# Sketched attention into a SiLU layer on one core: V loads on two queues, a new instruction order, and last chunks that come out token-major

## The chip, the core and the metric

The kernel runs on one core of a Trainium2 chip. The metric is device time in microseconds of one execution. Before the change it is 100.06 us, the median of four runs (98.99, 99.80, 100.32, 102.11). The profile shown is of the execution that took 98.99 us. Engines are called PE (TensorE matmul), PEld (its weight loads), DVE (VectorE), ACT (ScalarE), POOL (GpSimd) and SP (SyncE, which here only issues DMAs); ACT issues DMAs too, on a queue of its own.

## The reference

Four batches, four heads, 1088 tokens, head size 32. Attention without softmax: queries and keys are each projected by two 8 x 32 sketches, and the outer product of the two 8-vectors is a 64-vector of features. The result, as 4352 tokens of 128 values, goes through a layer of 2048 units with SiLU.

```python
def phi(x):
    a = np.einsum('rd,bhsd->bhsr', S1, x)
    b = np.einsum('rd,bhsd->bhsr', S2, x)
    return np.einsum('bhsi,bhsj->bhsij', a, b).reshape(*x.shape[:-1], r * r)
q_p, k_p = phi(q), phi(k)
kv = np.einsum('bhsf,bhsd->bhfd', k_p, v)
z = np.sum(k_p, axis=2)
num = np.einsum('bhsf,bhfd->bhsd', q_p, kv)
den = np.einsum('bhsf,bhf->bhs', q_p, z)[..., None] + 1e-06
x = (num / den).transpose(0, 2, 1, 3).reshape(4352, 128)
h = x @ w_in
out = (h / (1 + np.exp(-h))) @ w_out
```

## The kernel before

**Attention, per batch.** Of a batch's 1088 tokens, 1024 are eight blocks of 128 and 64 are a rest. K, Q and V are loaded by token groups (`load_x`, `load_k`, `load_v`, L174 to L192); four DMAs bring the V of one batch, one for each 32-partition group (c = 0 to 3). DVE transposes K and Q in 32 x 32 blocks (`KT`, L299; `QT`, L524, L527 and L594), PE projects them with masked sketch weights (L268), DVE transposes the projections back (`kab`, L316; `qabm`, L546, L618), and DVE or POOL forms the outer products (`kp`, L322; `qp`, L462, L638). V is cast to bf16 (`vcast`, which ends in `copy`, L161 on ACT and L163 on other engines). PE sums key features times V over the tokens (`kv0`, L350, for batch 0; `kv`, L372, for the others), and a masked copy of the sum is the key-value matrix `KV` (`kvm0`, L361 on ACT; `kvm`, `kvt`, `kvc` for the others). The denominator is folded into the queries: `z` (L328), `zt`, `l2` (L336) and `wm` (L340) make a matrix `WM`, `projm` (L539, L606) applies it, and the scale group (L454 to L457, or L630 to L633) multiplies, sums, inverts and scales. The query features are transposed, in batch 0 by PE (`pet`, L483, four 128 x 128 blocks with a copy `qt` after them), in the others by DMA (`dmat`, L644). The numerator matmul (L496, L650, L658) gives the attention result with its 128 values on the partitions, copied to `xT` (eight blocks) or `xR` (the rest of all batches).

**The layer.** `moe_tasks` (L708) takes a chunk of 512 or 256 tokens. For each piece of units, `h` (L718) fills a PSUM tile `H` of 128 x 1024, `silu` (L722, ACT) makes a bf16 tile `G` of it, and `o` (L729) adds `w_out` times `G` into one bank, with the 128 output values on the partitions. There are 68 such pieces. At a chunk's end `tro` (L734, DVE) transposes the bank in 32 x 32 blocks and the store writes it in four DMAs of 32 values (128 bytes) per row (`store_main`, L690); the rest of all batches, 256 tokens, goes out in eight (`store_rest`, L700). Chunks are called m, batch, first block: m34 and m36 are the last two of batch 3, of 256 tokens each, and mR is the rest. There are two `H` tiles, four other PSUM banks (`B`) and eight `G` tiles.

**What sets the order.** Every piece of work is a task of the class `Plan` (L45), with an engine or a choice of engines, a planned cost, tasks it depends on, and PSUM or `G` buffers that it takes and gives back. The text `ORDER` lists all task numbers by hand, with a `.n` where an engine is chosen. `replay` goes through the list with the planned costs, only to decide which free buffer each task gets; `emit` writes the instructions in the list's order, and each engine runs its own in that order, without overtaking. Where a planned PE gap ahead of the first `h` is left, `fill` (L837) puts matmuls of zeros there. SP runs its DMA issues in order too; eight DMA semaphores are used in turn, so an issue waits until the transfer that had its semaphore before has landed.

**Loads at the start.** SP issues K in four parts, Q in two, the four V loads, the next batch's K, the two halves of w_in, the first quarter of w_out and the next Q; the other quarters of w_out follow with later loads. The weights come as fp32 and are cast to bf16 in quarters by POOL or ACT (`cast_w`). ACT issues the two sketch loads (L200) ahead of its table load and a small warm-up activation.

```python
vc = [pl.add(("ACT", "POOL"), (...), lambda e, lo=lo, hi=hi: vcast(e, lo, hi), lv, ...)
      for lo, hi in ((0, CUT), (CUT, NBX))]
```

Each of the two casts of batch 0's V depends on all four loads (`lv`).

Of the kernel before, what the change touches and what calls it, by code (L numbers as in the profile page):

```python
# [9 lines left out]
FP32 = mybir.dt.float32  # L10
BF16 = mybir.dt.bfloat16
ACT = mybir.ActivationFunctionType
# [3 lines left out]
ORDER = """  # L16
0 6 73 27 24 1 28 23 2.1 21 3.1 29 32 22 4 96 30 33 7 5 31 10 34 39.1 15 41.0 36 101 35 54 49 47.0
74 55 50 51 57 75 45.1 43.0 52 58 25.0 56 77 37.0 78 76 59 26.0 60 42 38 142 40 44 61.0 13 46 48
139 66 53.1 67 62 141 97 63.0 9.0 17 103 8.1 68.1 64 99 104 65.0 100 19 79 11.0 225 80 98 228 226
12.0 144 69 182 105 229 140 70.1 86.1 231 143 107 71 106 232 234 81.1 72.1 87 121 113 235 239 14.0  # L20
114 82 240 88.1 108.0 242 83.1 115 89 227 146 16.0 90.0 84 245 116 110.0 85.0 147 122 243 123 111.0
124 246 253 125 18.0 241 126 254 244 127 248 247 249 102.0 230 256 148 130.0 257 20.0 259 128.0 233
131 260 236 250 237 109.0 262 129 251 265 149 263 255 112.0 150 258 238 145.0 152.1 266 117 164 156
118.1 268 151.0 119 252 271 269 120.0 261 190 91.1 264 272 189 154.0 134 184 274 136.1 137.0 183
267 155.0 185 157 270 275 153.1 186 279 132.1 273 280 276 305 277 158 306 282 159 278 191 283 165
193 285 192 167 308 198.0 286 166 168 160 309 169 199 170 288 161.1 307 200 289 311 310 312 281
171.0 291 284 292 173.0 314 172 162 287 315 317 197.0 174 290 318 294 293 295 133 201 320 202 313
163.1 194.1 321 323 187 196.1 316 319 324 195.0 297 177 298 188.0 326 180.1 296 327 179.1 300 322
175.0 301 207 325 331 299 332 334 92 302 335 93.1 357 303 208 358 304 135 360 211 328 210 361 363
329 209 364 337 330 212 359 338 213 366 94 333 367 176 340 336 341 95.1 343 218.0 216.0 203 219 344  # L30
369 339 204.0 370 217 214.0 346 362 347 205 349 206.0 215 138.1 342 350 372 365 373 221 178 375
181.1 224.1 345 376 409 368 410 412 220 413 378 222.1 371 379 223.1 352 411 353 414 383 374 384 386
348 387 389 377 390 380 392 381 385 393 395 382 351 396 398 354 399 401 355 388 402 404 356 391 405
415 394 416 397 423 400 424 426 403 427 418 406 419 429 407 417 430 437 408 420 438 440 421 425 441
422 432 428 433 443 431 444 446 434 447 439 435 442 436 445 448 449 450
# [9 lines left out]
class Plan:  # L45
# [29 lines left out]
    def replay(self, seq):  # L75
        now, mode, queue, port = dict(self.now), None, 4.2, 0.0
# [42 lines left out]
def kernel(  # L119
# [11 lines left out]
    nc = tc.nc  # L131
# [129 lines left out]
    def dma(kb, fn, deps=(), issue=0.44, lag=1.6, due=None, ready=0.0, eng="SP", rate=330.0, name=""):  # L261
        return pl.add(eng, issue, fn, deps, lag=lag, due=due, ready=ready, dq=kb / rate, name=name)
# [9 lines left out]
    def load(b):  # L272
# [13 lines left out]
        ks[b]["lv"] = [dma(139, lambda c=c: load_v(nc.sync, b, c), dv, due=at + 0.5, rate=250.0, name=f"lv{b}{c}") for c in range(4)]  # L286
        qs[b]["lq"] = dma(557, lq, dq, due=at + 1.0, name=f"lq{b}")

    def key_tasks(b, cuts):
# [102 lines left out]
        if b == 0:  # L392
            lv = [dma(139, lambda c=c: load_v(nc.sync, 0, c), due=5.0 + 0.1 * c, rate=250.0, name=f"lv0{c}") for c in range(4)]
# [46 lines left out]
        else:  # L440
            k1 = pl.add("PE", 0.42, kv, ou + vc, take=("s",), mode="32", name=nm("kv"))
            t = pl.add(("DVE", "ACT"), (0.23, 0.32), kvm, [k1], name=nm("kvm"))
            t = pl.add("PE", 0.12, kvt, [t], name=nm("kvt"))
# [142 lines left out]
    def query_tasks_hm(b):  # L586
# [94 lines left out]
        n0 = pl.add("PE", 0.32, num, dm[0:2] + [kst["kvd"]], take=("s", "s"), mode="64", name=nm("num"))  # L681
        n1 = pl.add("PE", 0.09, numr, [dm[2], kst["kvd"]], take=("s",), mode="64", name=nm("numr"))
        st["nums"] = [n0, n1]
        st["xs"] = [pl.add(both, (0.6, 0.62), lambda e, g=g: xcopy(e, g), [n0], give=[(n0, g)], name=nm(f"x{g}")) for g in range(2)]
        st["x8"] = pl.add(both, (0.28, 0.22), xrest, [n1], give=[(n1, 0)], due=T0 + STEP * (16 * b + 12), name=nm("xr"))

    def store_main(b, a0, na, queues):
        def f(ot):
            for r in range(4):
                queues[r % len(queues)].dma_start(  # L690
                    AP(tensor=out.tensor, offset=out[b * S + a0, 32 * r].offset,
                       ap=[[SA * DM, 32], [DM, na], [1, 32]]),
                    ot[32 * r: 32 * (r + 1), 0: 32 * na].rearrange("p (a y) -> p a y", y=32))
        return f

    def store_rest(ot):
        o = ot[:, 0: B * XN].rearrange("p (b c y) -> p b c y", c=NX, y=32)
        for r in range(4):
            for c in range(NX):
                nc.sync.dma_start(  # L700
                    AP(tensor=out.tensor, offset=out[4 * NB + c, 32 * r].offset,
                       ap=[[SA * DM, 32], [S * DM, B], [1, 32]]),
                    o[32 * r: 32 * (r + 1), :, c, :])
# [4 lines left out]
    def moe_tasks(x, n, xdeps, store, nst=4, tag=""):  # L708
# [15 lines left out]
        def o(jp, sl=None):  # L724
            if jp == 0:
                cc["o"] = sl
            for i in range(J):
                j = J * jp + i
                nc.tensor.matmul(cc["o"][:, :n], w_out[:, j, :], view(cc["g", jp], i),  # L729
                                 start=(j == 0), stop=(j == NJ - 1))  # L730
# [139 lines left out]
```

## Time and profile before

| What | Value |
|---|---|
| median of four runs | 100.06 us |
| profiled execution: its time / its span | 98.99 / 96.9 us |
| granted PE clock, mean | 0.982 |
| ACT: 68 SiLU tiles (L722) | 65.0 us, 1032 ns each |
| PE: `h` (L718) x160 / `o` (L729) x176 | 37.8 / 37.6 us |
| DVE / POOL busy | 58.3 / 29.8 us |
| chain of waits: PE / DVE share | 72% / 8% |
| DMA queue of SP: packets, data | 30240, 12.72 MB |
| output stores: 24 of 64 KB, 16 of 32 KB, 8 of 16 KB | 2.0, 1.7 to 1.8, 1.6 us to landing |

The page has busy times by engine, the busy share in 40 slices (2.4 us each), and the chain of waits, which follows the work that ended last back to the start. The timeline gives for each row its start and duration in us from the span's start, the engine (a `q` behind it means that its sequencer issues a DMA), the line, and the operation with its tiles as out<-in; `x4` means four instructions run together, and the bracket shows how long the engine stood idle before, and what ended that. Matmuls overlap, so the time of a matmul group is best read from the chain, where each piece counts once.

### The profile page before, as it was taken

The page shows a single profiled execution, that of the slowest core. Times are in us where ns is not written, and L with a number is a line of the kernel's source. Part 1 is how long each engine was busy: PE and PEld are TensorE (multiplying, and loading weights), DVE is VectorE, ACT ScalarE, POOL GpSimd, SP SyncE. Part 2 cuts the span into 40 slices and gives each one's busy share as a digit, 9 for nine tenths or more (in the row PEclk, how much of TensorE's full clock was granted, in tenths as well). Part 3 has the DMA queues.
Part 4 walks back from the last instruction along what each step waited for, and adds up shares of the span by engine and source line. Part 5 has one row for each costly group of instructions (what it writes and reads, how often), then busy time and mean ns, then how long its engine had stood idle before and what let it go on. Part 6 is the DMA issues. An engine that isn't in the chain of part 4 may idle for free.

```text
span 96.9 us, 2290 instructions
## 1 busy us (share of the span) xinstructions
PE 87.4 (90%) x879; PEld 51.5 (53%) x879; DVE 58.3 (60%) x146; ACT 71.9 (74%) x88; POOL 29.8 (31%) x41
## 2 busy tenths in 40 slices
PE   5998779999998699999999999999999999999600
PEld 4565369693755344454454443454564447799400
DVE  4586999977999997489953678992040220210200
ACT  3310176998587579888999998999999999999200
POOL 5029319799299995069000000000000000000000
PEclk9999999999999999999999999999999999999975
DMA  1999999999982854941086506727300166053151
GB/s 37 247 264 234 309 404 336 296 231 250 277 265 74 153 93 70 227 69 31 0 167 120 194 0 108 112 54 151 72 0 0 20 99 98 0 82 59 28 82 27
DMA packets 30874, 12.93 MB, mean 133 GB/s; under 512 B 26256, under 2 KB 29072, under 8 KB 30864
## 3 DMA queue, kind: packets, MB, share of 16 engines
q1 hardware_dynamic: 30240, 12.72, 56.2%
q8 instruction: 7, 0.11, 0.5%
q10 hardware_dynamic: 624, 0.07, 0.5%
q14 instruction: 3, 0.02, 0.1%
HBM read 8.79 MB, written 2.23 MB: 114 GB/s over the span
## 4 chain that ended last, share of the span: by engine, by line
PE 72%; DVE 8%; issue 1%; DVEq 0%
PE H L718 30%; PE B L729 27%; PE B L268 4%; DVE qp L638 4%; PE B L837 2%; PE B L372 1%; DVE aqs L633 1%; PE B L328 1%; PE B L606 1%; PE B L650 1%; PE B L483 1%; PE B L496 1%; DVE ot L734 1%; DVE den L631 1%; PE H L350 1%
## 5 line engine op out<-in xcount | busy, mean ns | idle before, releaser
L722 ACT ACTIVATE G<-H 128x1024 bf16<-128x1024 f32 x68 | 65.0, 1032 | 6.2 <-PE H L718 5.7
L729 PE MATMUL B<-G,w_out 128*128 128x512 bf16 (+1 forms) x176 | 37.6, 330 | 1.2 <-DVE ot L734 1.2
L718 PE MATMUL H<-xT,w_in 128*128 128x512 bf16 (+1 forms) x160 | 37.8, 338 | 0.0
L718 PEld LDWEIGHTS <-w_in 128*128 128x128 bf16 x176 | 18.4, 115 | 12.4 <-issue 3.6
L729 PEld LDWEIGHTS <-w_out 128*128 128x128 bf16 x176 | 17.0, 98 | 12.0 <-issue 1.5
L322 POOL TENSOR_TENSOR kp<-kab 128x512 bf16<-128x512 f32 (+1 forms) x15 | 16.7, 1137 | 9.1 <-DVE kab L316 9.1
L734 DVE STREAM_TRANSPOSE ot<-B 128x512 f32<-128x512 f32 (+1 forms) x11 | 6.4, 588 | 17.8 <-PE B L729 17.6
L837 PE MATMUL B<-zero 128*128 128x256 bf16 x51 | 8.7, 313 | 1.1 <-DVE fmask L231 1.1
L638 DVE TENSOR_TENSOR qp<-aqs,qabm 128x1024 bf16<-128x1024 f32 (+1 forms) x8 | 9.1, 1164 | 0.1
L299 DVE STREAM_TRANSPOSE KT<-Kx 128x576 f32<-128x576 f32 (+4 forms) x10 | 6.0, 615 | 2.4 <-DMA Kx<-in_k_dram 2.3
L837 PEld LDWEIGHTS <-zero 128*128 128x128 bf16 x51 | 5.2, 110 | 2.7 <-DVE fmask L231 1.0
L163 DVE CAST xT<-B 128x512 bf16<-128x512 f32 (+1 forms) x6 | 3.6, 631 | 3.9 <-PE B L650 3.9
L322 DVE TENSOR_TENSOR kp<-kab 128x512 bf16<-128x512 f32 (+1 forms) x6 | 4.3, 732 | 0.1
L594 DVE STREAM_TRANSPOSE QT<-Qx 128x1024 f32<-128x1024 f32 x3 | 3.7, 1236 | 0.7 <-DMA Qx<-in_q_dram 0.7
L462 POOL TENSOR_TENSOR qp<-aqs,qabm 128x512 bf16<-128x512 f32 (+1 forms) x4 | 3.8, 962 | 0.8 <-DVE aqs L457 0.8
L268 PE MATMUL B<-QT,WP 64*32 64x288 f32 (+1 forms) x64 | 3.3, 385 | 0.8 <-DVE QT L527 0.8
L163 POOL CAST Vh<-Vf 128x1152 bf16<-128x1152 f32 x3 | 3.4, 1142 | 1.8 <-DMA Vf<-in_v_dram 1.8
L161 ACT ACTIVATE Vh<-Vf 128x640 bf16<-128x640 f32 (+1 forms) x2 | 1.3, 674 | 3.2 <-DMA Vf<-in_v_dram 3.2
L633 DVE TENSOR_TENSOR aqs<-qabm,den 128x288 f32<-128x288 f32 x3 | 3.2, 1051 | 0.1
L316 DVE STREAM_TRANSPOSE kab<-B 128x288 f32<-128x288 f32 x6 | 2.5, 451 | 1.0 <-PE B L268 1.0
L618 DVE STREAM_TRANSPOSE qabm<-B 128x256 f32<-128x256 f32 x6 | 2.5, 422 | 0.8 <-PE B L268 0.8
L163 POOL CAST w_in<-w_inf 128x512 bf16<-128x512 f32 x3 | 1.9, 646 | 3.7 <-DMA w_inf<-in_moe_w_in_dram 3.7
(90 smaller groups left out, 67.4 us busy)
## 6 DMA issues: line engine op xcount, KB each, us to landing
Kx<-in_k_dram SPq DMA_DIRECT2D x3, 544.0 KB, 7.5
Qx<-in_q_dram SPq DMA_DIRECT2D x3, 544.0 KB, 4.8
out_dram<-ot SPq DMA_DIRECT2D x24, 64.0 KB, 2.0
Vf<-in_v_dram SPq DMA_DIRECT2D x8, 144.0 KB, 6.8
Vf<-in_v_dram SPq DMA_DIRECT2D x8, 128.0 KB, 6.0
w_inf<-in_moe_w_in_dram SPq DMA_DIRECT2D x2, 512.0 KB, 7.9
w_outf<-in_moe_w_out_dram SPq DMA_DIRECT2D x4, 256.0 KB, 7.4
out_dram<-ot SPq DMA_DIRECT2D x14, 32.0 KB, 1.7
```

The source lines that it names most:

```text
L163: eng.tensor_copy(out=out, in_=in_)
L268: nc.tensor.matmul(dst[p][32 * c: 32 * (c + 1), lo:hi], WPf[64 * p: 64 * (p + 1), :], srcT[64 * p: 64 * (p + 1), c, lo:hi], start=True, st ...
L299: nc.vector.transpose(out=KT[:, c:c + 2, 32 * lo: 32 * hi], in_=src.rearrange("p c a d -> p c (a d)"))
L322: eng.tensor_tensor(out=st["kp"][:, H * lo: H * hi], in0=_bc(a, 2, R), in1=_bc(bb, 1, R), op=ALU.mult)
L462: eng.tensor_tensor(out=st[f"qp{lo}"], in0=_bc(st["aqs"][:, H * lo: H * hi], 2, R), in1=_bc(bq.rearrange("p a (h r) -> p (a h) r", h=H), 1 ...
L633: nc.vector.tensor_tensor(out=st["aqs"], in0=grp(0), in1=_bc(st["den"], 1, R), op=ALU.mult)
L638: eng.tensor_tensor(out=st["qp", i], in0=_bc(st["aqs"][:, g0: g0 + n], 2, R), in1=_bc(grp(1)[:, g0: g0 + n], 1, R), op=ALU.mult)
L718: nc.tensor.matmul(view(sl, i), w_inj[:, (J * jp + i) // 4, (J * jp + i) % 4, :], x, start=True, stop=True)
L722: nc.scalar.activation(out=sl, in_=cc[jp], func=ACT.Silu)
L729: nc.tensor.matmul(cc["o"][:, :n], w_out[:, j, :], view(cc["g", jp], i), start=(j == 0), stop=(j == NJ - 1))
L734: nc.vector.transpose(out=cc["ot"][:, :n], in_=cc["o"][:, :n])
L837: nc.tensor.matmul(hold["bank"][:, 0:256], zero[:, 0:P], zero, start=True, stop=True)
```

## The change

- Two of the four V loads of batch 0 and of batch 1 (c = 2 and 3) are issued by ACT; in the new order those of batch 0 stand on ACT behind the warm-up activation, and those of batch 1 behind ACT's cast of a w_in quarter and behind the first `qt` copy.
- `ORDER` is written anew. Among much else: the first half of w_in is issued ahead of batch 1's K; three of the w_out quarters come behind batch 1's and 2's K and Q; batch 0's second V cast goes from ACT to POOL, one of its key products from DVE to POOL, and `KV` of batch 0 from ACT to DVE, where it follows both scale groups of the first half and the third transpose of `m` (L551); eight `h` tasks come ahead of the first `o`. POOL casts three quarters of w_out behind four of batch 1's key products.
- The chunks mR, m34 and m36 are computed token-major: `o` takes 128 tokens of `G` as the weights and 128 columns of `w_out` as the moving operand, so 8 matmuls of 128 columns stand for 4 of 256 and two banks are filled. Two copies (`cpo`, DVE or ACT) take the place of the transpose, and each store writes full rows of 128 values (512 bytes), in four DMAs a chunk, issued in pairs by SP or ACT. In the new order the last two pairs are shared: of m34 and of m36, one pair each goes to SP and one to ACT. mR's eight stores become four.
- Planned costs and DMA rates of `Plan` are changed a little; they act on the choice of buffers and the count of fill matmuls alone, which goes from 51 to 49.

```diff
-0 6 73 27 24 1 28 23 2.1 21 3.1 29 32 22 4 96 30 33 7 5 31 10 34 39.1 15 41.0 36 101 35 54 49 47.0
+6 27 28 0 1 2.1 3.1 29 32 73 23 24 21 22 30 7 96 10 101 33 139 31 41.1 4 34 39.0 5 36 35 45.0 47.0
...
-        now, mode, queue, port = dict(self.now), None, 4.2, 0.0
+        now, mode, queue, port = dict(self.now), None, 4.3, 0.0
...
-        ks[b]["lv"] = [dma(139, lambda c=c: load_v(nc.sync, b, c), dv, due=at + 0.5, rate=250.0, name=f"lv{b}{c}") for c in range(4)]
+        ks[b]["lv"] = [dma(139, lambda c=c: load_v(nc.scalar if b == 1 and c > 1 else nc.sync, b, c), dv, due=at + 0.5, rate=220.0,
+                           eng="ACT" if b == 1 and c > 1 else "SP", name=f"lv{b}{c}") for c in range(4)]
...
-            lv = [dma(139, lambda c=c: load_v(nc.sync, 0, c), due=5.0 + 0.1 * c, rate=250.0, name=f"lv0{c}") for c in range(4)]
+            lv = [dma(139, lambda c=c: load_v(nc.scalar if c > 1 else nc.sync, 0, c), due=5.0 + 0.1 * c, rate=230.0,
+                      eng="ACT" if c > 1 else "SP", name=f"lv0{c}") for c in range(4)]
...
+    def store_rows(b, a0):
+        def f(eng, ot, c):
+            eng.dma_start(AP(tensor=out.tensor, offset=out[b * S + a0 + c, 0].offset, ap=[[SA * DM, 32], [4 * DM, 2], [1, DM]]),
+                          ot[32 * c: 32 * (c + 1), 0: 2 * P].rearrange("p (t y) -> p t y", t=2))
+        return f
...
-        def o(jp, sl=None):
+        def o(jp, *sl):
             if jp == 0:
-                cc["o"] = sl
+                cc["o"] = sl[0]
+                cc["or"] = sl
             for i in range(J):
                 j = J * jp + i
+                if rows:
+                    for t, d in enumerate(cc["or"]):
+                        nc.tensor.matmul(d[:, 0:P], view(cc["g", jp], i)[:, P * t: P * (t + 1)], w_out[:, j, :],
+                                         start=(j == 0), stop=(j == NJ - 1))
+                    continue
                 nc.tensor.matmul(cc["o"][:, :n], w_out[:, j, :], view(cc["g", jp], i),
                                  start=(j == 0), stop=(j == NJ - 1))
...
+        def cpo(eng, t):
+            if "ot" not in cc:
+                cc["ot"] = op.tile([P, 512], FP32, name="ot", tag="ot")
+            copy(eng, cc["ot"][:, P * t: P * (t + 1)], cc["or"][t][:, 0:P])
...
+        if rows:
+            ts = [pl.add(("ACT", "DVE"), (0.3, 0.24), lambda e, t=t: cpo(e, t), [last], give=[(first, t)], due=due + 3.5 * STEP,
+                         name=f"{tag}cp{t}") for t in range(2)]
...
+        for i in range(2):
+            pl.add(("SP", "ACT") if end else ("SP",), (1.0, 1.0) if end else (1.0,),
+                   (lambda e, i=i: [store(e, cc["ot"], r) for r in (2 * i, 2 * i + 1)]) if end else
+                   (lambda i=i: [store(nc.sync, cc["ot"], r) for r in (2 * i, 2 * i + 1)]),
+                   ts, due=due + 6 * STEP, last=1.0, name=f"{tag}st{i}")
...
+            end = b == B - 1 and lo >= 4
+            moe_tasks(xT[b][:, P * lo: P * hi], P * (hi - lo), need, store_rows(b, 4 * lo) if end else store_cols(b, 4 * lo, 4 * (hi - lo)),
+                      rows=end, end=end, tag=f"m{b}{lo}")
```

## The prediction

> **What bounds the kernel now.** I read the page's busy rows first, then the chain of waits, then the timeline of the first 17 us and of the last 20, then the DMA rows.
>
> ```profile
> PE 87.4 (90%) x879; PEld 51.5 (53%) x879; DVE 58.3 (60%) x146; ACT 71.9 (74%) x88; POOL 29.8 (31%) x41
> PEclk9999999999999999999999999999999999999975
> ```
>
> PE works 90% of the span at full granted clock. From the first `h` matmul at 15.95 us to the last `o` matmul at 91.14 the chain of waits lies on PE except for one stretch, in which DVE's query products come last and PE waits until DVE frees a bank:
>
> ```profile
> 28.30 3.52 DVE qp L638 x2
> 31.82 0.37 DVE ot L734
> 32.19 0.04 issue
> 32.23 1.02 PE B L729 x4
> ...
> 88.47 0.48 PE H L718 x4
> 88.94 2.20 PE B L729 x20
> 91.14 0.02 issue
> 91.16 0.45 DVE ot L734
> ```
>
> The waits by engine give that hold as 1.2 us (PE B L729 on DVE ot L734). So the time is three pieces: the head until 15.95, 75.2 us of PE, and a tail of 5.7 us (91.14 to the span's end at 96.9). The head, in the timeline (start, duration, engine, line; in brackets idle time and what ended it):
>
> ```profile
> 9.23 0.71 DVE L524 STREAM_TRANSPOSE QT<-Qx 128x512 f32<-128x512 f32 x1 [0.71 <-DMA Qx<-in_q_dram]
> ...
> 11.80 1.25 ACT L161 ACTIVATE Vh<-Vf 128x640 bf16<-128x640 f32 x2 [3.20 <-DMA Vf<-in_v_dram]
> ...
> 13.69 0.52 ACT L361 ACTIVATE KV<-H,fmask 128x64 bf16<-128x64 f32 x2 [0.63 <-issue]
> 13.76 0.39 PE L483 MATMUL B<-identb,qp 128*128 128x128 bf16 x4
> ...
> 14.51 0.31 DVE L457 TENSOR_TENSOR aqs<-qabm,den 128x64 f32<-128x64 f32 x1
> ...
> 15.38 0.38 ACT L161 ACTIVATE xT<-B 128x256 bf16<-128x256 f32 x1
> ```
>
> DVE waited for the second part of Q, ACT for V; then KV and the transposed queries gate the first numerator, its copy `xT` and the first `h`. The tail, in the timeline: the last rest stores, then four plus two on SP and two on ACT.
>
> ```profile
> 86.71 4.65 SPq L700 DMA_DIRECT2D out_dram<-ot  x8
> ...
> 91.45 3.18 SPq L690 DMA_DIRECT2D out_dram<-ot  x6
> 91.65 0.84 ACTq L690 DMA_DIRECT2D out_dram<-ot  x2
> ```
>
> SP issues until 94.63, one store behind the other; the last begins near 94.2 and lands near 95.9 (1.7 us for a 32 KB store by the DMA rows); 1.0 us of closing follows.
>
> **The change part by part.** The sum is made against the profiled execution, 98.99 us (span 96.9), the lowest of four runs whose median is 100.06.
>
> *V on two queues.* Two of four V loads of batch 0 move to ACT's queue behind the warm-up activation, which ends at 3.18. On SP two issues go (4 took 1.85 us, so 0.9 us), and the first half of w_in now stands ahead of the next K. On ACT two issues of 0.46 (the two S loads took 0.92) fall into idle time: ACT has nothing before 5.72. The numerator's casts wait for all of V. The DMA share is 0.91, 0.87, 1.08 and 1.09 in the four 2 us windows from 2.0, so no room is seen for a second queue to go faster; what moves ahead only pushes something back. That is Q: V's half (256 KB) now goes beside Q's second part, which DVE waits for already. Call its delay d. From below 0, if the engines take the extra packets in gaps that the share doesn't show. From above 1.5: Q's 544 KB took 3.24 us from K's last landing (2.29 + 3.7) to its own (3.31 + 5.9), and 256 KB at that rate is 1.5. At the 245 GB/s that all queues moved in 8 to 10 us it is 1.05, which I take, being the rate of the engines and not of one transfer. V as a whole lands when it did. The two issues for batch 1 on ACT (0.46 each) stand before and after the first `qt` copy, where ACT waits for DVE and PE anyway; without that cover they cost 0.9.
>
> The Trainium skill's page "DMA: Bandwidth & Descriptors", section "Issuing engines are not separate DMA queues", says that DMAs started by several engines interleave on the same 16 DMA engines and that only issue time is saved. It speaks against this part, and the share rows agree; by the page alone d would be near 1 us, not 0.
>
> *The head's new order.* Half of V's cast goes to POOL (ACT 0.61 and POOL about 0.6 side by side for 1.25 in a row): worth 0.6. One key product (0.54) leaves DVE for POOL. KV goes from ACT (done 14.21) to DVE, but on DVE it now stands behind both first scale groups and a third `qabm` transpose. Start to start in the trace, from QT's second part: 0.76 to the next transpose, 0.43 two of these, 0.10 WM, 0.50 two more, 0.57 two of `m`, 1.09 first scale, 0.61 `qp`, 1.07 second scale, 0.34 the third `m`, 0.25 KV (0.18 to 0.31 for the nearest copies) = 5.72, so KV is done at 9.23 + 5.72 = 14.95 + d. What follows keeps its steps: 0.19 to the numerator, 0.41 to `xT`, 0.38, 0.19 to `h`: first `h` at 16.12 + d against 15.95. Part A = +0.17 + d = **+1.2** (0.2 to 1.7). V's earlier cast is worth nothing, since KV then waits for DVE.
>
> *The middle.* PE's work is the same instructions; one transposition (0.22) moves ahead of the first `h`. POOL now casts three w_out quarters behind batch 1's products (before: the first at 19.95, ahead of them), ACT the fourth after its eighth silu. I walked the engines in the new order with the trace's durations, from KV done at 16.0 and the first `h` at 17.1. DVE: two KT (1.36), the scale group (1.35): 18.7. POOL from there: products of 1.07, 1.05, 1.07, 2.10 and 0.6, then the first w_out cast (0.61): 25.2. PE before its first `o`: eight `h` (3.5), three numerators and two transpositions of 0.22, projections of 0.72, 0.93, 0.62 and 0.6, z and l2 (0.58), 8.1 in all, and some 0.6 of waits for DVE's QT, WM and copies: 25.8, so the cast is 0.6 early. Thirteen tasks later the key-value matmul of batch 1 and the `z` of batch 2 wait some 0.9 for DVE, which again has two query products (3.5 beside POOL's, as at 28.30) ahead. The old hold of 1.2 and 0.2 of waits near 22.5 go. Part B = 0.6 + 0.9 - 1.2 - 0.2 - 0.2 = **-0.1**. Bounds: -1.6 if nothing stalls, +2.4 by the POOL rival below. After 37 us the trace shows no PE hold, and the changed order has its transposes and V loads at least 2 us ahead of their users: 0.
>
> *Token-major chunks.* The three last 256-token chunks' 12 `o` tasks have 8 matmuls of 128 columns, weights changed each time, for 4 of 256. The nearest row is L483: 128 columns, new weights each, 4 in 0.22 us of the chain, 55 ns. 8 x 55 = 0.44, as 4 x 0.109 now. From above: L729's weight loads last 98 ns on their own; 96 x (98 - 55) = 4.1. From below 0, since as many columns stream. I take 0: L483 is the same shape, with its loads hidden.
>
> The Trainium skill's page "TensorE: Matmul & The Clock Gate", section "Back-to-back issue gap", gives about 81 ns per matmul for a stream of load and matmul pairs at 128 columns. By it the chunks would cost 96 x 26 ns = 2.5 us more, and the sum would be a loss; L483's 55 ns in this trace decides against it.
>
> *The tail.* From the last matmul (0): the m34 chunk ended at -1.77, its two DVE copies (0.25 each) at -1.25; SP stores two (-1.25 to -0.35), ACT two after the last silu (-1.0, as 90.13 to 91.14 now; 0.4 each) until -0.2. The last copies on DVE and ACT (0.3) end at 0.35. ACT issues two until 1.2. SP's two wait for the DMA slots of ACT's m34 stores, which land 1.6 after -1.0 and -0.6: issues at 0.6 and 1.05, landing 2.65, closing 1.0: 3.65 against 5.74. Part C = **-2.05**. Eight rest stores become four (4.65 us of SP, hidden behind PE but queued ahead of the last ones). Bounds: -0.9 if ACT's stores come out 0.55 later and each landing takes 2.0, as the 64 KB stores do; -2.6 if full rows land 0.5 sooner.
>
> Sum: 1.2 - 0.1 + 0 - 2.05 = **-0.95 us**: 98.0 for the profiled execution, **99.1** on the median of 100.06, from which the rivals are counted too.
>
> **The rivals.**
> 1. *Q isn't delayed and the holds go.* For it: a DMA share is time of packets, not proof that no gap is left. Then A = 0.2, B = -1.6, C = -2.05: -3.45, 96.6.
> 2. *POOL is late with w_out* (slower). At 28.70 two POOL products took 3.60, beside DVE's, against 2.10 at 22.10. If the four long products ahead of the w_out casts run so, the first `o` waits 4 x 0.75 - 0.6 = 2.4 more: sum +1.45, 101.5. It decides from 0.95 us of wait on. Against it: DVE runs mostly transposes then.
> 3. *Weight loads show in the last chunks* (slower). At 98 ns a pair +4.1: sum +3.15, 103.2; from 65 ns a pair on it is a loss. Against it: L483.
> 4. *The tail stays*: stores wait for one another's landings, C = -0.9, sum +0.2, 100.3. For it: DMA slots are reused within 2 us of their landing.
>
> **How the numbers follow.** Forecast 0.42, rival 1 0.24, rival 2 0.16, rival 3 0.08, rival 4 0.10. Two per cent, 2.0 us, is about what a measurement of this kernel can tell from no change. Faster by over 2% is most of rival 1 and the forecast's low edge (d under 0.3): 0.20 + 0.06 = 0.26. Slower by over 2% is rival 3 and half of rival 2, whose wait can add to a long d: 0.08 + 0.09 + 0.05 for other holds of an order changed throughout = 0.22. Within: 0.52. The forecast's own range is 97.9 to 100.4; with the rivals, leaving out rival 3 and the edges, **96.5 to 101.6**.
>
> **What would show it.** Right: the second QT transpose starts near 10.3, KV on DVE ends near 16.0, first `h` near 17.1; L734's matmuls 55 ns apart; last landing about 2.7 us after the last matmul and the tail 3.7. Wrong: QT at 9.3 (d is 0); PE waiting for POOL's w_out casts near 25; 80 ns or more between L734's matmuls; ACT held at the fourth w_out cast; a stretch after 37 us in which PE waits for a transpose or for V.

## The result, and the profile after

The changed kernel takes 96.97 us (median of 22 runs, 95.81 to 98.25) beside 100.19 us for the kernel before (32 runs): ratio 0.973, 95% interval 0.970 to 0.976. Ratios, here and below, leave out the runs of a slower state, those over 1.5% above the fastest of their kernel, so they are not the quotients of these medians. The profiled execution took 96.27 us with a span of 93.9. So the time falls by about 2.7 us where the sum said 0.95.

The page of the changed kernel, busy rows and granted clock, to be held against the two rows shown of before:

```profile
PE 87.3 (93%) x925; PEld 51.8 (55%) x925; DVE 54.9 (58%) x147; ACT 71.9 (77%) x87; POOL 31.4 (33%) x43
PEclk9999999999999999999999999999999999999999
```

PE has the same busy time in a shorter span: what went away is time in which PE stood still. Where, is read in three places. The head, in the timeline:

```profile
1.74 0.41 ACTq L190 DMA_DIRECT2D Vf<-in_v_dram  x1
...
9.69 0.71 DVE L527 STREAM_TRANSPOSE QT<-Qx 128x512 f32<-128x512 f32 x1 [0.64 <-DMA Qx<-in_q_dram]
...
11.33 0.74 ACT L162 ACTIVATE Vh<-Vf 128x640 bf16<-128x640 f32 x1 [2.18 <-DMA Vf<-in_v_dram]
...
14.98 0.25 DVE L366 TENSOR_TENSOR KV<-H,fmask 128x128 bf16<-128x128 f32 x1
...
15.72 0.38 ACT L162 ACTIVATE xT<-B 128x256 bf16<-128x256 f32 x1 [0.73 <-PE B L499]
```

Q's second transpose starts 0.46 later than before (9.23) and `xT` is copied 0.34 later; the first `h` starts at 16.24 instead of 15.95. V's first load on ACT was issued at 1.74, beside the table load (1.68 to 2.96), not behind the warm-up activation, where the description of the change puts both; the second went out at 3.49. The middle, in the chain of waits:

```profile
25.65 0.47 DVE aqs L636
26.12 0.02 issue
26.15 2.36 DVE qp L641 x2
28.51 0.34 DVE kab L318
28.85 4.75 DMA qt<-qp
```

The two query products of batch 1 take 2.36 where they took 3.52, and no hold of PE follows on `ot`. What POOL does beside them, in the timeline, and the waits of PE after the first `h`, before:

```profile
28.70 3.60 POOL L322 TENSOR_TENSOR kp<-kab 128x512 bf16<-128x512 f32 x2
...
PE B L729 <- DVE ot L734: 1.2, 1, 1.2
```

and changed:

```profile
27.72 1.79 POOL L164 CAST Vh<-Vf 128x1152 bf16<-128x1152 f32 x1 [2.08 <-DMA Vf<-in_v_dram]
...
PE B L374 <- DVE kp L324: 0.4, 1, 0.4
PE B L653 <- DMA qt<-qp: 0.2, 1, 0.2
```

(A row of waits gives the sum in us, the number of waits and the longest.) The last matmul ends at 90.46 instead of 91.14, so the middle is 74.2 instead of 75.2. PE idles for 0.7 of it instead of 1.3 and is busy for 73.5 instead of 73.9, since 0.4 of its work now stands ahead of the first `h`. The tail, in the timeline:

```profile
88.71 0.49 DVE L164 COPY ot<-B 128x128 f32<-128x128 f32 x2 [2.05 <-PE B L734]
89.23 2.52 SPq L698 DMA_DIRECT2D out_dram<-ot  x4
89.23 0.86 ACTq L698 DMA_DIRECT2D out_dram<-ot  x2
90.44 0.29 DVE L164 COPY ot<-B 128x128 f32<-128x128 f32 x1 [1.24 <-PE B L734]
90.50 0.28 ACT L162 ACTIVATE ot<-B 128x128 f32<-128x128 f32 x1 [1.08 <-DMA out_dram<-ot]
90.82 0.80 ACTq L698 DMA_DIRECT2D out_dram<-ot  x2
```

SP and ACT issue side by side; the last store lands at 92.80 and the span ends 3.44 us after the last matmul, where it was 5.74. (The very last chunk is now m34, the one ahead of it m36.) So the span changes by +0.3 in the head, -1.0 in the middle and -2.3 in the tail, 3.0 in all, of which 0.3 goes back outside the span (2.1 before, 2.4 now).

All profiles of the study, in us (QT: start of Q's second transpose; tail: from the end of the last matmul to the end of the span, good to 0.05). The profiles of e1 and of e12 to e16 have a dip of the granted clock between 11 and 40 us (mean 0.951 to 0.983); of these only what lies outside the dip is used, and their last matmuls are not compared. Nor is that of e7, whose profile is of an execution of 98.14 us, 1.9 above the fastest of that kernel.

| Kernel | Ratio to before | 95% interval | QT | first `h` | last matmul | tail |
|---|---|---|---|---|---|---|
| before | 1 | | 9.23 | 15.95 | 91.14 | 5.74 |
| changed | 0.973 | 0.970 to 0.976 | 9.69 | 16.24 | 90.46 | 3.44 |
| e1 column tail | 0.990 | 0.981 to 0.999 | 9.89 | 17.21 | 92.69 | 4.9 |
| e2 V on SP | 0.975 | 0.959 to 0.991 | 8.31 | 15.33 | 90.02 | 3.5 |
| e3 tail alone | 0.993 | 0.986 to 1.000 | 8.84 | 16.96 | 91.81 | 4.2 |
| e4 order alone | 0.996 | 0.988 to 1.004 | 7.90 | 15.06 | 90.19 | 5.3 |
| e5 POOL beside | 0.987 | 0.982 to 0.992 | 9.46 | 16.01 | 92.51 | 3.5 |
| e6 V1 first | 0.978 | 0.971 to 0.985 | 10.20 | 16.74 | 91.43 | 3.5 |
| e7 V all on SP | 0.970 | 0.961 to 0.978 | 8.80 | 16.87 | 92.24 | 3.5 |
| e8 changed again | 0.969 | 0.961 to 0.977 | 9.74 | 16.76 | 90.26 | 3.4 |
| e9 rows, one queue | 0.982 | 0.973 to 0.990 | 9.73 | 16.75 | 90.53 | 4.5 |
| e10 as e2 | 0.969 | 0.960 to 0.979 | 8.80 | 16.71 | 90.91 | 3.5 |
| e11 changed, third | 0.981 | 0.975 to 0.986 | 9.48 | 16.02 | 91.05 | 3.5 |
| e12 V on ACT alone | 1.005 | 1.000 to 1.010 | 9.44 | 16.67 | 92.46 | 5.7 |
| e13 half the fillers | 0.965 | 0.957 to 0.973 | 9.63 | 16.11 | 90.66 | 3.7 |
| e14 e13, V on SP | 0.974 | 0.968 to 0.981 | 8.16 | 15.39 | 94.09 | 3.7 |
| e15 before, half the fillers | 1.009 | 1.003 to 1.015 | 8.81 | 15.91 | 94.02 | 6.0 |
| e16 one gap | 0.985 | 0.978 to 0.991 | 9.93 | 17.18 | 92.78 | 3.5 |
| e17 e16, V on SP | 0.983 | 0.977 to 0.988 | 8.41 | 14.96 | 90.71 | 3.6 |
| e18 columns, last two | 0.989 | 0.973 to 1.006 | 9.13 | 15.68 | 89.52 | 4.2 |

Between one kernel's own repeats (changed, e8, e11) the ratio moves by 0.012, so ratios tell apart only differences of over 1 us; smaller ones are read from the stages.

### The profile page after: what moved, and what is told of

Read it like the earlier page. It is cut to its first block, busy times and chain, and to the rows that moved or that the text cites. A ratio compares the mean times of both kernels' runs of the same rounds, so it can differ in the third digit from the quotient of the medians.

```text
span 93.9 us, 2381 instructions
## 1 busy us (share of the span) xinstructions
PE 87.3 (93%) x925; PEld 51.8 (55%) x925; DVE 54.9 (58%) x147; ACT 71.9 (77%) x87; POOL 31.4 (33%) x43
## 4 chain that ended last, share of the span: by engine, by line
PE 62%; DVE 14%; DMA 13%; SPq 2%; ACT 2%; issue 2%; DVEq 0%
PE H L720 26%; PE B L737 19%; DMA Qx<-in_q_dram 7%; DMA qt<-qp 5%; DVE qp L641 4%; PE B L734 4%; PE B L269 3%; ACT G L724 2%; PE B L609 2%; SPq L186 2%; DVE kp L324 2%; PE B L858 2%; DMA out_dram<-ot 1%; DVE kab L318 1%; PE B L486 1%
## 5 line engine op out<-in xcount | busy, mean ns | idle before, releaser
L737 PE MATMUL B<-G,w_out 128*128 128x512 bf16 (+1 forms) x128 | 30.9, 352 | 0.0
L737 PEld LDWEIGHTS <-w_out 128*128 128x128 bf16 x128 | 12.4, 97 | 10.3
L742 DVE STREAM_TRANSPOSE ot<-B 128x512 f32<-128x512 f32 (+1 forms) x8 | 5.1, 643 | 12.7 <-PE B L737 10.4
L164 POOL CAST Vh<-Vf 128x1152 bf16<-128x1152 f32 (+1 forms) x4 | 4.7, 1173 | 15.6 <-DMA Vf<-in_v_dram 9.2
L858 PE MATMUL B<-zero 128*128 128x256 bf16 x49 | 8.5, 315 | 1.1 <-DVE fmask L232 1.1
L301 DVE STREAM_TRANSPOSE KT<-Kx 128x512 f32<-128x512 f32 (+4 forms) x10 | 5.9, 610 | 2.1 <-DMA Kx<-in_k_dram 2.1
L734 PE MATMUL B<-w_out,G 128*128 128x128 bf16 x96 | 6.5, 219 | 0.0
L858 PEld LDWEIGHTS <-zero 128*128 128x128 bf16 x49 | 4.9, 111 | 2.7 <-DVE fmask L232 1.0
L734 PEld LDWEIGHTS <-G 128*128 128x128 bf16 x96 | 5.9, 98 | 0.5
L164 DVE COPY ot<-B 128x128 f32<-128x128 f32 x5 | 1.3, 287 | 5.2 <-PE B L734 5.2
L465 POOL TENSOR_TENSOR qp<-aqs,qabm 128x512 bf16<-128x512 f32 x3 | 3.2, 1070 | 2.7 <-DVE aqs L460 2.7
L324 DVE TENSOR_TENSOR kp<-kab 128x512 bf16<-128x512 f32 x4 | 3.6, 894 | 0.0
```

Of the source, the lines that this page charges most:

```text
L164: eng.tensor_copy(out=out, in_=in_)
L301: nc.vector.transpose(out=KT[:, c:c + 2, 32 * lo: 32 * hi], in_=src.rearrange("p c a d -> p c (a d)"))
L324: eng.tensor_tensor(out=st["kp"][:, H * lo: H * hi], in0=_bc(a, 2, R), in1=_bc(bb, 1, R), op=ALU.mult)
L734: nc.tensor.matmul(d[:, 0:P], view(cc["g", jp], i)[:, P * t: P * (t + 1)], w_out[:, j, :], start=(j == 0), stop=(j == NJ - 1))
L742: nc.vector.transpose(out=cc["ot"][:, :n], in_=cc["o"][:, :n])
L858: nc.tensor.matmul(hold["bank"][:, 0:256], zero[:, 0:P], zero, start=True, stop=True)
```

## The experiments: the tail

**e1, columns again.** The matmuls of L734, their two copies and the row stores go; order and queues stay.

```diff
-                if rows:
-                    for t, d in enumerate(cc["or"]):
-                        nc.tensor.matmul(d[:, 0:P], ...)
...
-            copy(eng, cc["ot"][:, P * t: P * (t + 1)], cc["or"][t][:, 0:P])
+            if t == 0:
+                nc.vector.transpose(out=cc["ot"][:, :n], in_=cc["o"][:, :n])
...
-            moe_tasks(..., store_rows(b, 4 * lo) if end else store_cols(b, 4 * lo, 4 * (hi - lo)),
+            moe_tasks(..., store_cols(b, 4 * lo, 4 * (hi - lo)),
```

> The changed kernel with its three last chunks computed column-major again (four matmuls of 256 columns, one DVE transpose of 128x256, column stores of 32 KB, eight rest stores), with the new order and the new split of the stores over SP's and ACT's queues kept. Theory (the split and the order carry the tail, the form of the chunk little): PE's last matmuls as long as before, tail 3.4 to 3.9 us, 0 to 0.5 us over the changed kernel, so a ratio of 0.973 to 0.978 to the kernel before. Rival (full rows carry it): tail 4.5 us or more, ratio 0.983 or more. If the token-major matmuls cost PE anything, the stretch up to the last matmul gets shorter here; by theory it stays within 0.1 us.

Measured: tail 4.9, so the theory fell and the rival's number came. But its waits on SP's queue in the last 14 us show a mechanism that neither had:

```profile
SPq L692 <- DMA out_dram<-ot: 2.6, 1, 2.6
```

Eight completion semaphores serve the stores of both queues, and a store waits until the one that had its semaphore before it has landed. In the traces they go round in turn, but not in the order of the program: ACT's last stores have theirs ahead of some of SP's that stand before them in `ORDER`. With eight rest stores instead of four the turn is shifted, and SP's last store of m30 has the semaphore of a store that ACT issued at 91.47. SP stood 2.6 us for it (in the changed kernel its longest such wait ahead of a store is 0.9), and the last stores went out at 94.93.

**e18, columns in the last two chunks only.** As e1, but the rest chunk keeps rows and four stores, which was meant to keep the turn of the semaphores.

```diff
-                if rows:
+                if rows and tag == "mR":
...
+            elif t == 0:
+                nc.vector.transpose(out=cc["ot"][:, :n], in_=cc["o"][:, :n])
...
-            moe_tasks(..., store_rows(b, 4 * lo) if end else store_cols(b, 4 * lo, 4 * (hi - lo)),
+            moe_tasks(..., store_cols(b, 4 * lo, 4 * (hi - lo)),
```

> The changed kernel with the two last 256-token chunks column-major again (column stores, one DVE transpose each), the rest chunk left in full rows with its four stores, so that the stores of the two last chunks use the same completion semaphores in the same turn as in the changed kernel. Theory (the 1.45 us that the tail lost in the first experiment came from four rest stores more, which turned the eight semaphores so that SP stood 2.6 us for a store of ACT's queue): tail 3.6 to 4.1, no wait of SP of over 1.2 us for a landing; last matmul as in the changed kernel; ratio 0.972 to 0.980. Rival (column stores themselves are the cost): tail 4.6 or more, ratio 0.983 or more.

Measured: tail 4.2, SP's longest wait for a landing 1.3. That lies between the two theories. But the turn was not quite kept: in the trace SP's second store of the last chunk but one has the semaphore of ACT's first store of that chunk (issued at 88.30, landed at 90.14), which it does not have in the changed kernel, and the 1.3 is its wait for that. So of the 1.45 that e1 lost, about half is the turn of the semaphores; how the rest (4.2 against 3.44) divides between this wait and the columns themselves is not shown.

**e9, rows on one queue.** Two choices in the order: `463.1` and `448.1` become `463.0` and `448.0`.

> The changed kernel with its full rows, but all stores of the two last chunks on SP's queue. Theory (rows and the second queue are each worth about as much): SP issues eight stores from 89.2 us on, 0.4 to 0.5 us each, so the last is issued near 92.8 and lands 1.2 later; tail 4.3 to 5.0 instead of 3.45, ratio 0.978 to 0.988. Rival (the rows carry the tail, the second queue is worth nothing): tail 3.4 to 3.7.

Measured: tail 4.5; SP issues eight stores in 3.60 us from 89.29. No store waits for a landing here. As the theory had it: the second queue is worth 1.0.

**e3, the tail alone in the kernel before.**

```diff
+                queues[c // 2].dma_start(
+                    AP(tensor=out.tensor, offset=out[b * S + a0 + c, 0].offset, ap=[[SA * DM, 32], [4 * DM, 2], [1, DM]]), ...)
...
-                moe_tasks(..., store_rest, 8, tag="mR")
+                moe_tasks(..., store_rest, 4, rows=True, tag="mR")
```

> The kernel before with the new tail alone: its three last chunks token-major, stored in full rows, the rest chunk by four stores on SP, the two last chunks by two stores on SP and two on ACT each; order and loads as before. Theory (the tail's gain stands by itself): head and middle unchanged within 0.2 us, tail 3.4 to 3.8 instead of 5.74, ratio 0.977 to 0.981. Rival (the tail's gain comes with the new order, which has the rest stores out of the way 5 us earlier): tail 4.5 or more, ratio 0.988 or more.

Measured: tail 4.2, between theory and rival: 1.5 of the 2.3 come with the rows and the queues. The other 0.8 need not be the place of the rest stores in the order: before its first store of the last chunk but one SP stands 2.0 us for a store of ACT's. The ratio is 0.993, a gain of 0.7; in the profiled execution the first `h` came 1.0 later than before (see the fillers below), but whether that holds for the other runs is not known.

**e4, the order alone.** V on SP, columns, eight rest stores, and the old split of the stores (`463.0`, last chunk in turn on SP and ACT), in the new order.

> The changed kernel with only its new order: all V loads on SP, the three last chunks column-major, the rest chunk by eight stores and the last but one by four on SP, the last one's four in turn on SP and ACT, as in the kernel before. Theory: head 0 to 0.4 us shorter than in the changed kernel, middle 1.0 us shorter than before, tail 3.9 to 4.8 (the rest stores no longer stand ahead of the last ones); ratio 0.974 to 0.985. Rival (the order brings the middle only, the tail needs its own changes): tail 5.5 or more, ratio 0.988 or more.

Measured: tail 5.3, the rival's side: the order by itself takes 0.4 off the tail. Here too SP stands 1.5 us for a store of ACT's. Its longest such wait is 0.9 in the changed kernel, 1.3 in e18, 1.5 in e4, 2.0 in e3 and 2.6 in e1. So the tail's gain is shown for rows, second queue and order together, and for the second queue by e9; what rows and order are worth without these waits is not shown.

## The experiments: the middle

**e5, POOL kept busy.** Two scratch products on POOL ahead of batch 1's V cast; nothing uses them.

```diff
+            for i in range(2 if b == 1 else 0):
+                nc.gpsimd.tensor_tensor(out=scr[i], in0=_bc(w_inf[:, 0:64].rearrange("p (g r) -> p g r", r=R), 2, R),
+                                        in1=_bc(w_inf[:, 64:128].rearrange("p (g r) -> p g r", r=R), 1, R), op=ALU.mult)
```

> The changed kernel with two scratch products more on POOL (128x512 bf16 from 128x512 f32, the shape of its key products, results not used), put where POOL waits for V of batch 1, just after its third w_out cast, while DVE makes the two query products of batch 1. Theory (DVE's products are slow beside POOL's products, and were fast in the changed kernel because POOL stood still): DVE's aqs 1.2 to 1.4 us instead of 0.46 and its two query products 3.2 to 3.7 together instead of 2.45; the scratch products 1.6 to 2.0 each; POOL's cast of V 1 us or more later, and a hold of PE of 0.5 to 1.5 us comes back near 30 us: ratio 0.98 to 0.99. Rival (the two engines don't disturb each other; the products were slow in the kernel before for another reason): aqs 0.46, products 1.23 each, scratch products 1.07 each and so just within POOL's wait: no change, ratio 0.973.

The timeline of e5 where DVE makes the products:

```profile
25.42 0.74 DVE L640 TENSOR_TENSOR aqs<-qabm,den 128x288 f32<-128x288 f32 x1
26.19 3.52 DVE L645 TENSOR_TENSOR qp<-aqs,qabm 128x1024 bf16<-128x1024 f32 x2
26.60 4.04 POOL L393 TENSOR_TENSOR scr<-w_inf 128x512 bf16<-128x512 f32 x2
...
31.69 4.73 POOL L325 TENSOR_TENSOR kp<-kab 128x512 bf16<-128x512 f32 x5
```

and its waits of PE:

```profile
PE B L375 <- POOL Vh L164: 1.0, 1, 1.0
...
PE B L375 <- POOL kp L325: 0.8, 1, 0.8
```

3.52 us again, to the hundredth what the kernel before took. Singly, a DVE product beside a POOL product takes 2.08 (1.22 alone) and POOL's 2.05 (1.06 alone): side by side the pair takes about as long as one after the other (2.28). The last matmul comes 2.1 to 2.3 later than in the changed kernel and e8, and the ratio 0.987 lies above its neighbour e8's 0.969. The theory holds for the products. The holds of PE are now for POOL, which the two scratch products make late, so e5 does not show what the slower products alone cost at the end. The page "GPSIMD Engine Reference" of the Trainium skill (section "Key points") says that GpSimd shares its SBUF interfaces with VectorE and contends with DVE instructions that have two SBUF inputs; these rows agree and add the price.

**e6, batch 1's V first.** In the order, `97 98` move ahead of `141 140`.

> The changed kernel with SP's two V loads of batch 1 moved ahead of two V loads of batch 2, so that V of batch 1 lands near 23 instead of 27.6 us and POOL doesn't wait for it after its w_out casts. Theory of contention: POOL's cast and key products now run beside DVE's aqs and query products of batch 1, which take 1.2 or more and 3.2 or more; the hold of PE for DVE's transposes near 30 us comes back in part, against kv of batch 1 being ready sooner: last matmul 0 to 0.8 us later than in the changed kernel. Rival (the middle was won because nothing is late): V sooner makes the key-value matmul of batch 1 sooner and takes the wait of 0.4 us with it: last matmul 0 to 0.5 us earlier.

The timeline of e6:

```profile
25.96 1.14 POOL L145 CAST Vh<-Vf 128x1152 bf16<-128x1152 f32 x1
...
26.57 0.84 DVE L617 TENSOR_TENSOR aqs<-qabm,den 128x288 f32<-128x288 f32 x1
27.07 1.27 POOL L305 TENSOR_TENSOR kp<-kab 128x512 bf16<-128x512 f32 x1
27.45 3.11 DVE L622 TENSOR_TENSOR qp<-aqs,qabm 128x1024 bf16<-128x1024 f32 x2
```

V sooner put POOL's work back beside DVE's: 3.11 instead of 2.36, and a last matmul 1.0 later than in the changed kernel (Q came 0.5 later too). After the first `h`, PE has one wait: 1.0 for `qt<-qp`, the transfer behind these products, where the changed kernel has 0.2. Nothing speaks for the rival. In the changed kernel V of batch 1 lands at 27.6 because its two SP loads are issued at 19.92 and 20.64; POOL stands for it from 25.64 to 27.72, and just then DVE works alone.

## The experiments: the head

**e2 and e10, V of batch 0 on SP; e7, of both batches.** e8 and e11 are the changed kernel itself, run beside them.

```diff
-            lv = [dma(139, lambda c=c: load_v(nc.scalar if c > 1 else nc.sync, 0, c), ..., eng="ACT" if c > 1 else "SP", ...)
+            lv = [dma(139, lambda c=c: load_v(nc.sync, 0, c), ...)
```

> The changed kernel with all four V loads of batch 0 on SP's queue, in the same place in the order. Theory (V beside Q delays Q by 0.46 us, and V is early enough either way): the second QT transpose starts at 9.2 instead of 9.7, V lands after it, first h 0 to 0.4 us earlier, ratio 0.969 to 0.973. Rival (the second queue is worth having because V comes in sooner): V's casts end a microsecond or more later, KV waits for V instead of for DVE, first h 0.4 us or more later, ratio 0.977 or more.

> The changed kernel with all V loads of the first two batches on SP's queue. Theory (V's first load on ACT's queue is issued at 1.74 us, goes ahead of parts of K and of Q, and the head pays): QT2 starts 0.8 to 1.5 us sooner than in the changed kernel of the same set, first h 0.5 to 1.0 sooner, last matmul 0.3 to 0.9 sooner, ratio 0.965 to 0.972. Rival (the difference was one of the chip or of the run, the transfers share the engines the same way): within 0.3 us of the changed kernel of the same set at QT2 and at h.

> The changed kernel as it is, as the neighbour of the other three on the same chip: QT2 at 9.6 to 9.9, first h 16.2 to 16.6, aqs 0.46 and query products 1.23 each, tail 3.4; ratio 0.970 to 0.976. If QT2 comes at 8.3 or sooner, loads vary between runs by as much as the first experiment with V on SP showed, and that experiment proves nothing.

> The changed kernel with all four V loads of batch 0 on SP's queue, once more, beside the changed kernel on the same chip. Theory (V on ACT's queue delays Q by 1.4 us against the same order with V on SP, and part of that reaches the end): QT2 near 8.3, 0.3 to 0.9 us faster than the changed kernel, ratio 0.964 to 0.970. Rival (the head's gain is taken back by later waits): within 0.2 us of the changed kernel.

> The changed kernel as it is, as the neighbour of the other three: ratio 0.970 to 0.976, QT2 at 9.5 to 9.9. First h at 16.2 if TensorE's fillers run at 109 ns from 5.4 us on, near 16.8 if they still run at 213 ns until 9 us.

Measured: QT at 8.31, 8.80 and 8.80 with V on SP, at 9.69, 9.74 and 9.48 with V on ACT: 1.0 us between the means. V's load on ACT lands ahead of K's third part and pushes it and Q back: K's third part lands at 4.3 to 4.5 with V on SP and at 5.2 to 6.0 with V on ACT, Q's first at 6.7 to 7.0 and at 7.4 to 8.3. (e14, below, also with V on SP, has K's third part at 5.2, but Q's first at 6.4.) Yet the times don't tell the two apart: in four pairs, each run on one chip, the ratio with V on SP is lower by 0.012 (e10 beside e11) and 0.002 (e17 beside e16), the same within 0.001 (e7 beside e8) and higher by 0.009 (e14 beside e13). So the theories are right about the transfers, and a gain in time is not shown. The first `h` shows why some of the cases cannot differ. TensorE in e8:

```profile
7.59 2.10 PE L858 MATMUL B<-zero 128*128 128x256 bf16 x9
9.62 0.61 PE L330 MATMUL B<-kab 128*32 128x32 f32 x18
```

and in the changed kernel's first profile:

```profile
7.33 1.16 PE L858 MATMUL B<-zero 128*128 128x256 bf16 x9
8.41 0.51 PE L330 MATMUL B<-kab 128*32 128x32 f32 x18
```

L858 is `fill`. Its matmuls follow one another every 213 ns at first and every 109 ns later. The step came between 4.2 and 5.9 us in 15 of 20 profiles and between 9.2 and 10.5 in five (e3, e7, e8, e9, e10); in all of these but e10 the key sums, behind the fillers, still take 0.60 to 0.69 instead of 0.51. Where it is late, nine fillers take 2.10 instead of 1.16, the key sums and Q's projection wait behind them, and the first `h` comes at 16.7 to 17.0 in all five, V on SP or not. Where it is early, V on ACT costs 0.7 to 0.9 at the first `h` (16.24 and 16.02 against e2's 15.33).

**e12, V on ACT alone in the kernel before.** The same edit of `lv`, the other way.

> The kernel before with one part of the change alone: the third and fourth V load of batch 0 on ACT's queue; order, loads of batch 1 and tail as before. Theory (V ahead of Q costs the head and V's own earlier landing gives little): the second QT transpose 0.5 to 1.0 us later than 9.0, V's cast 0.4 to 0.7 sooner than 11.8, first h 0.2 to 0.8 us later; ratio 1.000 to 1.008. Rival (V gates the head in the kernel before, so V sooner is a gain): first h 0.3 us or more sooner, ratio 0.997 or less.

Measured: ratio 1.005 (1.000 to 1.010); QT at 9.44, V's cast at 11.22 instead of 11.80. V comes sooner, Q later, and nothing is gained; a cost of up to 1% is within the interval. The first `h`, at 16.67, lies behind the dip and decides nothing.

**e13 to e17, fewer fillers.** e13, e14 and e15 take half of them away after 4.6 us, from the changed kernel, from it with V on SP, and from the kernel before; e16 and e17 do it in one gap only, with V on ACT and on SP.

```diff
-        step = 0.213 if lo < 4.6 else 0.11
+        step = 0.213
```

> The changed kernel with about half the filler matmuls (on zeros, result not used) after 4.6 us. Theory (in some executions TensorE steps to its full rate only at 9.2 us instead of near 5; fillers planned at 110 ns then take 213 ns each and hold the key sums and Q's projection up by about 0.9 us, whatever V does): where the step is late, first h at 16.0 to 16.3 instead of 16.75; where it is early, as before at 16.0 to 16.3; the times spread less, ratio 0.966 to 0.972. Rival (fewer fillers keep the clock low for longer): fillers at 213 ns beyond 9.3 us, first h 17 or later, slower than the changed kernel.

> The changed kernel with V of batch 0 on SP's queue and about half the fillers after 4.6 us. Theory (Q's delay by V on ACT's queue counts only where the fillers don't hold PE longer): QT2 near 8.3, first h 15.3 to 15.8 whether the step is early or late, 0.3 to 0.8 us faster than with the half of the fillers alone; ratio 0.960 to 0.967. Rival (the later stages give the head's gain back): within 0.2 us of the run with half the fillers alone.

> The kernel before with about half the fillers after 4.6 us. Theory: its head too is held by fillers where the step is late (first h 16.96 there, 15.95 otherwise); now 15.8 to 16.2 in both, 0.2 to 0.6 us faster in the median, ratio 0.993 to 0.998. Rival: no difference, since V and not PE gates this head.

> The changed kernel with five of nine fillers less in one gap only, that between the two key projections' transposes (planned 6.6 to 7.6 us, seen at 7.3 to 8.2 or, at 213 ns, at 7.6 to 9.3); the later gaps stay filled. Theory: the late step of TensorE's rate costs the head 0.5 us less and the clock stays up later, since the gaps after 10 us are filled: first h 16.0 to 16.4 in either case, no clock dip at 11 to 15 us, ratio 0.966 to 0.972. Rival (every filler left out lets the clock fall later): fillers at 213 ns again after 10 us, a dip in the granted clock, ratio 0.975 or more.

> The same with V of batch 0 on SP's queue. Theory: Q comes 1.4 us sooner and the fillers don't hide it: first h 15.2 to 15.9, last matmul 0.3 to 0.6 us sooner than in the run before this one, ratio 0.962 to 0.968. Rival (V's queue makes no difference that reaches the end): within 0.2 us of the other.

Measured: with fewer fillers the matmuls of e13 fell back to 213 ns at 12 to 14.7 us, those of e15 at 14 to 14.5, those of e16 at 12.7 to 13.7. e13 still has its theory's first `h` (16.11) and a ratio no worse than the changed kernel's (0.965); e16 goes its rival's way (first `h` at 17.18, 0.985). V on SP adds nothing to either: e14 is at 0.974, e17 at 0.983. e15 is 0.9% slower than before (interval 1.003 to 1.015), and e15's granted clock is 0.947 to 0.986 over 12 runs, that of the kernel before 0.967 to 0.996 over 17. But e1, with all its fillers, fell back at 12.4 too: 0.983 or less in six of its 12 runs, where e13 and e16 have that in two of six. So the fillers are not the only condition; that they earn their time is shown for the kernel before alone. e17 kept its rate and had the earliest head of all, 14.96, and still its last matmul came at 90.71. Its waits of PE:

```profile
PE B L737 <- POOL w_out L164: 1.4, 2, 0.9
```

The first `o` pieces waited for POOL's casts of w_out: the prediction's second rival. Of the early heads in the new order (e2, e4, e14, e17) this is the only one that met it; e12 and e15, in the old order, wait 2.0 for the same casts.

## Why the prediction was wrong in its size

It had the direction, the tail and the wide range (96.5 to 101.6; its own, 97.9 to 100.4, lies above), gave 0.26 to a gain of over 2%, and lost 1.8 us in two steps.

*Part A, +1.2; measured +0.3.* "At the 245 GB/s that all queues moved in 8 to 10 us it is 1.05": against the same order with V on SP the delay is 1.0, as taken. The path is another: V was to go beside Q's second part, but its first load went out beside K's third and moved Q by moving K, so the size is in part luck. And it was added to the QT time of the kernel before, 9.23, and the new order with V on SP has Q at 7.9 to 8.8. Why that is sooner than before (8.81 to 9.23 in three profiles), though SP issues the same first loads at the same times, these runs don't settle. In the two profiles compared d is 0.46 (-0.59 against the sum), and the steps from there to `h` took 6.55 instead of 6.89 (-0.34).

The step that failed beneath it: every microsecond at the first `h` was counted as one at the end. In eight profiles of the changed order with its tail (changed, e2, e8, e9, e10, e11, e17, e18) the first `h` lies between 14.96 and 16.76, and the last matmul between 89.5 and 91.1 without following it: 90.71 for the earliest head, 90.26 for the latest. Between the two, PE idles 2.0 and 1.1 us after the early heads of e17 and e2, 0.7 to 1.1 after the late ones of e8, e9 and e10; and it is busy for 73.8 and 73.6 against 72.8 to 73.1, since with a late head more of its other work stands ahead of the first `h`. (e11, whose head lies between, idles 1.8, so this is no strict rule.) An early PE meets w_out's casts (1.4 in e17) or the transfer of `qt` (0.9 in e2); a late one finds them done. That the landing times of the loads set this pace is likely (a quarter of w_out lands at 24.2 to 24.7 in the changed kernel, e2, e4, e7 and e8 alike), but no run here was made to move them.

*Part B, -0.1; measured -1.0.* "DVE, which again has two query products (3.5 beside POOL's, as at 28.30)": the overlap was assumed, and V's landing for batch 1, which decides when POOL starts its next products, was not followed through SP's queue. POOL stood until 27.72, and DVE took 0.46 and 2.36 instead of 1.34 and 3.52. Of the 1.5 that the sum has for new waits of PE (0.6 and 0.9), 0.4 and 0.2 came; and 0.4 of PE's work, not 0.2, moved ahead of the first `h`. e5 and e6 put the overlap back: DVE's products take 3.52 and 3.11 and the last matmul comes 1.0 to 2.3 later, behind POOL itself in e5, behind DVE's products (PE waits 1.0) in e6.

*Token-major chunks, 0: right.* Eight L734 matmuls take 0.45 to 0.46 in the chain, 56 ns each. The 81 ns that the Trainium skill's page "TensorE: Matmul & The Clock Gate", section "Back-to-back issue gap", gives for such pairs do not show here.

*Part C, -2.05; measured -2.30: right in mechanism.* The last store landed 2.34 after the last matmul instead of 2.65, because SP's last two went out at +0.50 and +0.90 instead of +0.6 and +1.05, and ACT's last landed 1.6 after its issue at +0.71.

*Rivals.* The first (96.6) had the sum that came, for the wrong reason: Q was delayed, but the holds went. The fourth is what e1 looks like. The third did not occur.

## What to carry to other kernels

Before a delay at the head is added to a sum, look for what else PE will meet later on (casts, loads with their own landing times): a head that comes sooner or later by a microsecond moved the end of this kernel by nothing that shows in the scatter of its profiles. When DVE's products look slow in a profile, see what POOL does beside them, and follow the loads that decide when POOL is there. With stores on two queues, look in the trace which stores share a completion semaphore: one queue can stand for the other's store, and a few stores more or less far ahead change which.

## What the runs showed of the hardware

- DVE and POOL products side by side take 2.08 and 2.05 us, alone 1.22 and 1.06; a POOL cast beside DVE's `aqs` makes that 0.74 to 1.34 instead of 0.46.
- TensorE's step from 213 to 109 ns for 256 columns came near 5 us or, in five of 20 profiles, between 9.2 and 10.5, while the page's granted clock reads full speed in both. The Trainium skill's page "TensorE: Matmul & The Clock Gate", Part 1, says that the activity window runs free and the step moves by about 0.5 us with it; here it moved by over 4.
- ACT issues a DMA while its table load runs (1.74 inside 1.68 to 2.96), and a load on its queue takes its share at once: V's 128 KB, issued beside K's third part, landed ahead of it (5.71 against 5.96).
